# Two feed-forward blocks behind an attention: GpSimd kept to the attention, two-bank product tiles, one operation for both halves, and reordered products

## The chip, the cores and the metric

One core of one Trainium2 chip runs the kernel. The metric is the device time of one execution in microseconds. TensorE (PE, with its weight loads shown apart as PEld) multiplies, VectorE (DVE), ScalarE (ACT) and GpSimd (POOL) work element by element, and SyncE (SP) issues nearly all transfers.

## What is computed

```python
x = attention(q, k, v, w_phi)           # (2304, 512), feature-map attention
h = x @ w_in                            # w_in (512, 2048)
x = (relu(h) ** 2) @ w_out              # w_out (2048, 512)
gate = sigmoid(x @ w_gate)              # w_gate, w_val (512, 1536)
out = (gate * (x @ w_val)) @ w_out2     # w_out2 (1536, 512)
```

All inputs and outputs are fp32. The first block is called h below, the second gv.

## The kernel before

**Numbers in two parts.** Each fp32 operand of a matmul is split into a high part `hi` that TensorE takes and the rest `lo = a - hi`; three passes (hi·hi, hi·lo, lo·hi) make one product. ACT writes `hi` as a copy and another engine subtracts. For weights that is `wsplit` (L128): ACT at L131, the subtraction at L132 on POOL or DVE, as `on_pool` (L707) decides by the weight's name. For activations it is `split` (L85), with the subtraction on DVE at L90.

**Stages.** The 2304 tokens are three blocks of `TB` = 768 columns. The attention comes first. For token block 0, `h0_step` (L493) then multiplies directly with 16 pieces of `w_in`, and `o1_step` (L508) accumulates `g @ w_out` two steps behind it. For blocks 1 and 2 of the first feed-forward block, and for all three of the second, a `chain` of 2x2 block products with seven multiplications in place of eight makes `h`, or gate and value; 16 steps `o1` (first) or 12 steps `o2` (second) follow. One product is 12 matmuls of 384 columns; its two halves (m = 0, 1) have one PSUM bank each.

**A chain.** For each group q the seven products p1, p2, p6, p7, p5, p3, p4 (L600 to L626) go to three accumulators: X for p1, p6, p5, p3, Z for p2, Y for p7, p4. After p1, p6 and p5 `keep` (L569) has ACT copy both halves of X to scratch at L572, before the next product may add to X. After p2, p5 and p4 `joined` (L574) has DVE add Z or Y at L577; `squared` (L585) and `gated` (L595) make g of it. All this is done half by half.

**Around the products.** `xops` (L530) prepares the seven inputs of the next token block at one step of o1 or o2, its differences on POOL (L544). `g_split` (L632) splits a piece of g at the start of the step that uses it. While the h chains run, `weight` (L98) converts weights from their input format with four DVE operations (L105, L106, L107, L110) and one of ACT (L109), and `sums` (L152) adds and subtracts pieces of them on POOL (L156 to L159); the results go to DRAM and are fetched again.

**Order.** Each engine and each queue works strictly in its own order. The code's order is a proposal: a scheduler with a timeline of its own puts the instructions of each engine into a row when the kernel is built. `run_ahead(first[k], 11, 6)` (L712) fetches weights up to 11 products ahead and splits them up to 6 ahead.

**Buffers.** PSUM is one pool of eight single banks, `bank` (L56). `gx` has 16 tiles for g and its parts, `sc` 10 scratch tiles of one bank's size.

## Time and profile before

| | us |
|---|---|
| median of 3 runs | 1064.37 (1063.57 to 1067.43) |
| the profiled execution's own time | 1063.96 |
| its span, first to last instruction | 1062.1 |
| PE busy | 1006.6 |
| DVE busy | 805.9 |
| ACT busy | 590.3 |
| POOL busy | 496.3 |

The time outside the span is 1.86 us. A line such as L565 stands for all instructions of that line of the kernel. The idle time of an engine is counted before an instruction, with the instruction that ended the wait behind an arrow. An engine's busy time counts overlapping instructions once.

### The profile page before, as it was taken

What the parts mean: (1) busy time and instruction counts of PE and PEld (TensorE: products, weight loads), DVE (VectorE), ACT (ScalarE), POOL (GpSimd) and SP (SyncE); (2) the same over time, 40 slices, a digit from 0 to 9 for tenths busy, and PEclk for the clock granted to TensorE, in tenths of its full rate; (3) what the DMA queues carried; (4) which work ended last, traced back from release to release, by engine and by line L of the source; (5) the groups of instructions that cost most, each with busy time, mean ns of one, the idle gap of its engine ahead of it and who ended that gap; (6) DMA issues with size and microseconds to landing.
All of it is one profiled execution on the core that took longest, in us unless ns stands there. A gap on an engine that the chain in (4) does not pass through costs nothing.

```text
span 1062.1 us, 18013 instructions
## 1 busy us (share of the span) xinstructions
PE 1006.6 (95%) x6488; PEld 869.9 (82%) x6488; DVE 805.9 (76%) x1218; ACT 590.3 (56%) x1220; POOL 496.3 (47%) x486
## 2 busy tenths in 40 slices
PE   8999999899998997599997999999999999999997
PEld 6666666687876997488996889998899997899986
DVE  7899997599985999893899966999545687365650
ACT  7888878344434665343564436666345674365630
POOL 4555655534647657664558652129302265111430
PEclk9999999999999998799998999999999999999999
DMA  9445422058876565355572664772254432444401
GB/s 247 119 139 155 149 64 90 30 209 306 287 250 185 180 200 158 124 181 178 182 227 80 197 210 139 233 244 89 80 151 135 125 97 75 132 128 132 120 19 60
DMA packets 117849, 162.20 MB, mean 153 GB/s; under 512 B 12928, under 2 KB 75008, under 8 KB 117760
## 3 DMA queue, kind: packets, MB, share of 16 engines
q1 hardware_dynamic: 117120, 160.20, 48.4%
q8 instruction: 51, 0.84, 0.3%
q10 hardware_dynamic: 640, 0.85, 0.2%
q14 instruction: 38, 0.31, 0.1%
HBM read 127.99 MB, written 33.03 MB: 152 GB/s over the span
## 4 chain that ended last, share of the span: by engine, by line
PE 52%; DVE 8%; issue 1%; ACT 1%; DMA 0%; ACTq 0%; DVEq 0%
PE a L565 29%; PE a L660 12%; PE a L519 11%; DVE xs L90 3%; DVE glo L90 1%; DVE G L593 1%; DVE c L577 1%; DVE G L598 1%; DVE w L106 0%; DMA wf<-wd 0%; DVE w L105 0%; DVE hl L132 0%; DVE w L110 0%; ACT c L572 0%; DVE w L107 0%
## 5 line engine op out<-in xcount | busy, mean ns | idle before, releaser
L132 POOL TENSOR_TENSOR hl<-wf,hl 128x512 fp32r<-128x512 f32 x168 | 251.7, 1507 | 414.2 <-ACT hl L131 387.2
L565 PE MATMUL a<-xs,hl 128*128 128x384 f32 x2184 | 387.6, 340 | 9.1 <-DVE c L577 4.8
L565 PEld LDWEIGHTS a<-xs,hl 128*128 128x128 f32 x2184 | 383.2, 191 | 12.5 <-ACT c L572 6.0
L131 ACT ACTIVATE hl<-wf 128x512 fp32r<-128x512 f32 x282 | 172.2, 627 | 114.9 <-PE a L660 33.9
L519 PE MATMUL a<-ghi,hl 128*128 128x256 f32 (+1 forms) x768 | 194.6, 342 | 0.5 <-DVE ghi L89 0.5
L132 DVE TENSOR_TENSOR hl<-wf,hl 128x512 fp32r<-128x512 f32 x114 | 87.7, 777 | 95.7 <-ACT hl L131 95.5
L519 PE MATMUL a<-glo,hl 128*128 128x512 f32 (+1 forms) x384 | 131.6, 345 | 23.7 <-DVE glo L90 23.7
L519 PEld LDWEIGHTS a<-ghi,hl 128*128 128x128 f32 x768 | 135.8, 192 | 17.3 <-issue 0.9
L660 PE MATMUL a<-hl,ghi 128*128 128x512 f32 x432 | 132.4, 395 | 0.0
L577 DVE TENSOR_TENSOR c<-c,a 128x384 f32<-128x384 f32 x156 | 83.2, 549 | 37.4 <-ACT c L572 25.0
L109 ACT ACTIVATE st<-st 128x512 f32<-128x512 f32 x68 | 46.6, 686 | 106.7 <-DVE w L106 105.5
L572 ACT ACTIVATE c<-a 128x384 f32<-128x384 f32 x156 | 73.1, 487 | 55.1 <-PE a L565 54.7
L519 PEld LDWEIGHTS a<-glo,hl 128*128 128x128 f32 x384 | 74.0, 193 | 34.6 <-DVE glo L90 25.6
L660 PEld LDWEIGHTS a<-hl,ghi 128*128 128x128 f32 x432 | 81.1, 188 | 19.5
L311 POOL PARTITION_ALL_REDUCE m<-qe x64 | 82.0, 1351 | 29.0 <-ACT qe L309 29.0
L660 PE MATMUL a<-hl,glo 128*128 128x512 f32 x216 | 82.1, 396 | 1.5 <-DVE glo L90 1.5
L501 PE MATMUL a<-xs,hl 128*128 128x512 f32 (+1 forms) x384 | 72.9, 346 | 6.9 <-ACT c L504 6.2
L501 PEld LDWEIGHTS a<-xs,hl 128*128 128x128 f32 x384 | 60.5, 191 | 18.7 <-ACT c L504 8.5
L87 ACT ACTIVATE ghi<-G 128x768 fp32r<-128x768 f32 x48 | 40.2, 839 | 63.4 <-DVE glo L90 51.7
L90 DVE TENSOR_TENSOR glo<-G,ghi 128x768 fp32r<-128x768 f32 x48 | 57.8, 1206 | 16.3 <-ACT ghi L87 13.7
L106 DVE SCALAR_TENSOR_TENSOR w<-st,w 128x512 uint32<-128x512 uint32 x68 | 63.0, 927 | 0.8
L110 DVE SCALAR_TENSOR_TENSOR w<-st,w 128x512 f32<-128x512 f32 x68 | 57.1, 841 | 4.6 <-ACT st L109 2.1
(106 smaller groups left out, 1377.1 us busy)
## 6 DMA issues: line engine op xcount, KB each, us to landing
wf<-wd SPq DMA_DIRECT2D x84, 256.0 KB, 2.9
wf<-smd SPq DMA_DIRECT2D x72, 256.0 KB, 3.3
st<-in_moe_w_out_dram SPq DMA_DIRECT2D x28, 512.0 KB, 5.1
wf<-wid SPq DMA_DIRECT2D x56, 256.0 KB, 4.9
wf<-gvd SPq DMA_DIRECT2D x54, 256.0 KB, 3.2
st<-in_moe_w_in_dram SPq DMA_DIRECT2D x16, 512.0 KB, 5.5
wf<-ismd SPq DMA_DIRECT2D x32, 256.0 KB, 3.7
wd<-w SPq DMA_DIRECT2D x28, 256.0 KB, 2.6
```

The costliest lines, as they stand in the source:

```text
L90: last_g[0] = nc.vector.tensor_tensor(lo, src, f(hi), ALU.subtract)
L106: nc.vector.scalar_tensor_tensor(b, hi, 0xC0000000, b, ALU.bitwise_and, ALU.bitwise_or)
L110: nc.vector.scalar_tensor_tensor(a, h, TINY, a, ALU.is_ge, ALU.mult)
L131: nc.scalar.activation(d[:, 0], a, AF.Copy)
L132: eng.tensor_tensor(d[:, 1], a, f(d[:, 0]), ALU.subtract)
L311: nc.gpsimd.partition_all_reduce(m, a[:, 1, :], channels=P, reduce_op=bass_isa.ReduceOp.absmax)
L501: nc.tensor.matmul(pp, lhsT=w[:, x, j, :], rhs=xs[j][:, y, o:o + n], start=k == 0, stop=k == 3 * NJ - 1)
L519: nc.tensor.matmul(acc[j][i], lhsT=w[:, x, j, :], rhs=a[y][:, o:o + n], start=c == 0 and k == 0 and (i == 0 or j % 2 == 0), stop=c == C1 - ...
L565: nc.tensor.matmul(acc[k][m], lhsT=w[:, i, 2 * m + kt, :], rhs=v[:, j, kt, :], start=start and n == 0, stop=n == 5, skip_group_check=True)
L572: nc.scalar.activation(side[name][m], acc["X"][m], AF.Copy)
L577: last_g[0] = nc.vector.tensor_tensor(a[m], a[m], acc[k][m], ALU.add)
L660: nc.tensor.matmul(acc[u], lhsT=g[x][:, u * P:(u + 1) * P], rhs=w[:, y].rearrange("p j f -> p (j f)"), start=c == 0 and n == 0, stop=c == ...
```

## The change

- POOL no longer subtracts for `wsplit`, nor for `sums`, nor for the differences of a token block: DVE does all three. `on_pool` goes. POOL keeps its work in the attention.
- From the end of the attention PSUM is a pool `pd` of four tiles of two neighbouring banks, and both halves of a product lie in one of them. `keep`, the joins, the squares and the splits each become one operation over 2x384 columns. The accumulators are one per group q (`acc["X", q]`).
- In the first block the join and relu become one custom DVE operation, `TENSOR_ADD_SAT` (max(min(a + b, 3e38), 0)); ACT squares.
- In `h0_step` both halves have 384 columns (before 512 and 256); ACT writes the high part as a square, squares once more in fp32, and DVE subtracts once.
- p1 of the next group is written ahead of p3, and p2 of the next group behind p4.
- The inputs of the next token block are made one by one over seven steps (`xop`). `g_split` for step c + 2 stands behind step c, the first two some products ahead of the chain's end. `gx` shrinks from 16 to 4 tiles, `sc` is 7 tiles of two halves.
- Weights of the second block are converted at an even pace (`converts2`).

```diff
-    ps = ctx.enter_context(tc.tile_pool(name="ps", bufs=8, space=PSUM))
+    pctx = ctx.enter_context(ExitStack())
+    ps = pctx.enter_context(tc.tile_pool(name="ps", bufs=8, space=PSUM))
...
-        eng.tensor_tensor(d[:, 1], a, f(d[:, 0]), ALU.subtract)
+        nc.vector.tensor_tensor(d[:, 1], a, f(d[:, 0]), ALU.subtract)
...
-        eng = nc.gpsimd.tensor_tensor
+        eng = nc.vector.tensor_tensor
...
+    pctx.close()
+    pd = ctx.enter_context(tc.tile_pool(name="pd", bufs=4, space=PSUM, reuse_waits="tile"))
-    gx = ctx.enter_context(tc.tile_pool(name="gx", bufs=16, reuse_waits="tile"))
-    sc = ctx.enter_context(tc.tile_pool(name="sc", bufs=10, reuse_waits="tile"))
+    gx = ctx.enter_context(tc.tile_pool(name="gx", bufs=4, reuse_waits="tile"))
+    sc = ctx.enter_context(tc.tile_pool(name="sc", bufs=7, reuse_waits="tile"))
...
+        r, sq = scr(), scr()
+        nc.scalar.activation(r, pp[:, :, :NH], AF.Relu)
+        nc.scalar.activation(gs[c][0], flat(r), AF.Square)
+        nc.scalar.activation(sq, r, AF.Square)
+        last_g[0] = nc.vector.tensor_tensor(gs[c][1], flat(sq), f(gs[c][0]), ALU.subtract)
...
-                nc.gpsimd.tensor_tensor(d[kt], x[kt], y[kt], ALU.subtract)
+            nc.vector.tensor_tensor(d, x, y, ALU.subtract)
...
+            a = (xp if i < 4 else xb).tile([P, 2, 2, NH], F32R, tag=f"xo{i}", name="xs")
+            split(a[:, 0], a[:, 1], src, nc.scalar)
...
-        side[name] = [scr(NH) for m in range(2)]
-        for m in range(2):
-            nc.scalar.activation(side[name][m], acc["X"][m], AF.Copy)
+        side[name, q] = scr()
+        nc.scalar.activation(side[name, q], acc["X", q], AF.Copy)
...
+    def squared(q, e, j, k, name=None):
+        dst = g_pair(q, e)[:, :, j * NH:(j + 1) * NH]
+        if name is None:
+            r = scr()
+            nc.scalar.activation(r, acc[k, q], AF.Relu)
+        else:
+            r = side.pop((name, q))
+            last_g[0] = nc.vector._custom_dve(TENSOR_ADD_SAT, out=r, in0=r, in1=acc[k, q], s0=BIG, s1=0.0)
+        nc.scalar.activation(dst, r, AF.Square)
...
+            nc.vector.tensor_tensor(a, a, acc[k, q], ALU.add)
...
     def o1(t, c):
-        g_split(c)
         o1_step(t, c, take(("o1", t, c)))
+        g_ahead("h", c + 2)
...
+            order += [(p6, "s2", q), (p7, "s3", q), (p5, "s1", q)]
+            if q < n - 1:
+                order.append((p1, "a11", q + 1))
+            if q == n - 1:
+                order.append((p2, "a12", q))
+            order += [(p3, "s4", q), (p4, "a22", q)]
+            if q < n - 2:
+                order.append((p2, "a12", q + 1))
...
+    def g_ahead(kind, c):
+        if kind == "h" and c < C1:
+            q, r = divmod(c, 4)
+            g_split(c, q, *divmod(r, 2))
...
+        for i, (fn, k, q) in enumerate(order):
+            if i == len(order) - 7:
+                act(0.0, g_ahead, kind, 0)
+                act(0.0, g_ahead, kind, 1)
...
-            if c == C1 // 2:
-                act(0.0, xops, (t + 1) % nblk)
+            if 0 <= c - 3 < 7:
+                act(0.0, xop, (t + 1) % nblk, ORDER[c - 3])
...
-        upto = int(ngv * (at + 4) / (moe2 - 6)) if at < moe2 else ngv + int((at - moe2 + 4) / 3)
+        upto = int(NW2 * (at + 6) / (moe2 + 36))
```

Three places show how the rows of an engine move.

POOL, where the attention ends. Before, weight splits (`hl`, L132) and the sums of weights (`s`, L156 to L159) follow the attention's own `m` and `rc`:

```order
L311 ISA m<-qe 128x288 x4
L132 ISA
L132 TENSOR_TENSOR hl<-wf,hl 128x512 x3
L404 COPY rc<-rd 32x9 x8
L132 TENSOR_TENSOR hl<-wf,hl 128x512 x3
L404 COPY rc<-rd 32x9 x16
L132 TENSOR_TENSOR hl<-wf,hl 128x512 x4
L156 TENSOR_TENSOR s<-wf 128x256
```

After, these are POOL's last rows:

```order
L318 ISA m<-qe 128x288 x4
L411 COPY rc<-rd 32x9 x8
L318 ISA m<-qe 128x288 x4
L411 COPY rc<-rd 32x9 x24
L837 UNCONDITIONAL_BRANCH
L837 ISA
```

None of the splits and sums is left on POOL; they stand in DVE's row.

DVE in the first steps of o1 for token block 1. Before (`xs`: split of an input of the next block, `glo`: low part of g, `w`: conversion of a weight, `c`, `G`: joins and squares):

```order
L577 TENSOR_TENSOR c<-c,a 128x384
L90 TENSOR_TENSOR xs<-u,xs 128x384 x2
L593 SCALAR_TENSOR_TENSOR G<-c 128x384
L106 SCALAR_TENSOR_TENSOR w<-st,w 128x512
L90 TENSOR_TENSOR xs<-c,xs 128x384
L110 SCALAR_TENSOR_TENSOR w<-st,w 128x512
L593 SCALAR_TENSOR_TENSOR G<-c 128x384
L90 TENSOR_TENSOR xs<-c,xs 128x384 x3
L107 SCALAR_TENSOR_TENSOR w<-st,w 128x512
L90 TENSOR_TENSOR glo<-u,ghi 128x768
L90 TENSOR_TENSOR xs<-c,xs 128x384 x3
```

After, at the steps 4 to 6 of the same o1 (`c<-u`: difference of two pieces):

```order
L112 TENSOR_SCALAR w<-st 128x512
L97 TENSOR_TENSOR xs<-u,xs 128x768
L139 TENSOR_TENSOR hl<-wf,hl 128x512
L113 SCALAR_TENSOR_TENSOR w<-st,w 128x512
L114 SCALAR_TENSOR_TENSOR w<-st,w 128x512
L97 TENSOR_TENSOR glo<-G,ghi 128x768
L97 TENSOR_TENSOR xs<-u,xs 128x768
L112 TENSOR_SCALAR w<-st 128x512
L139 TENSOR_TENSOR hl<-wf,hl 128x512
L117 SCALAR_TENSOR_TENSOR w<-st,w 128x512
L113 SCALAR_TENSOR_TENSOR w<-st,w 128x512
L97 TENSOR_TENSOR glo<-G,ghi 128x768
```

A `glo` now stands behind every four to eight other operations, and the seven `xs` lie between them one at a time.

PE in the chain of token block 1, group 1. Before, from p5 to p4 (`a_5001` and `a_5002` are the halves of X, `a_5192` and `a_5193` Z of the next group's p2, `a_5070` and `a_5071` the halves of Y; `xs_4652`, `xs_4657` and `xs_4666` are the inputs of p5, p3 and p4):

```order
L565 MATMUL a_5001<-xs_4652,hl_4962 128x384 x6
L565 MATMUL a_5192<-xs_4625,hl_5067 128x384
L565 MATMUL a_5002<-xs_4652,hl_4962 128x384 x6
L565 MATMUL a_5192<-xs_4625,hl_5067 128x384 x3
L565 MATMUL a_5193<-xs_4625,hl_5067 128x384 x4
L565 MATMUL a_5001<-xs_4657,hl_4998 128x384 x6
L565 MATMUL a_5070<-xs_4666,hl_5021 128x384 x6
L565 MATMUL a_5002<-xs_4657,hl_4998 128x384 x6
```

After, the same group (`d_4832` is X, `d_5054` Z of the next group, `d_4980` X of the next group, `d_4940` Y; `xs_4556` is the input of p5, `xs_4606` of p3, `xs_4611` of p4):

```order
L590 MATMUL d_4832<-xs_4556,hl_4849 128x384 x12
L590 MATMUL d_5054<-xs_4331,hl_4937 128x384 x12
L590 MATMUL d_4832<-xs_4606,hl_4897 128x384 x12
L590 MATMUL d_4980<-xs_4415,hl_4955 128x384 x7
L590 MATMUL d_4940<-xs_4611,hl_4918 128x384 x12
```

Between p5 and p3 stood 7 matmuls of the next p2 after p5's last one; now all 12 of it stand there, and p5 is one row of 12.

## Rows read from the trace of the kernel before

**Rows 1.** The page: the span, and busy time by engine.

```profile
span 1062.1 us, 18013 instructions
PE 1006.6 (95%) x6488; PEld 869.9 (82%) x6488; DVE 805.9 (76%) x1218; ACT 590.3 (56%) x1220; POOL 496.3 (47%) x486
```

**Rows 2.** Busy time in seven stages: PE, PEld, DVE, ACT, POOL, granted clock, DMA.

```profile
0.00:196.98 196.98, 188.61 (x2121) 124.80 (x2121) 164.65 (x363) 156.18 (x385) 111.79 (x188) 1.00 0.46 134
196.98:350.45 153.47, 141.34 (x770) 120.58 (x769) 128.44 (x180) 63.91 (x126) 82.52 (x82) 0.97 0.65 216
350.45:500.39 149.94, 132.56 (x723) 121.48 (x723) 126.05 (x145) 74.05 (x142) 89.83 (x69) 0.93 0.56 177
500.39:639.83 139.44, 129.51 (x722) 119.75 (x721) 119.55 (x140) 71.81 (x135) 84.38 (x62) 0.98 0.55 174
639.83:780.04 140.21, 138.79 (x721) 127.81 (x721) 110.72 (x165) 82.14 (x160) 49.28 (x32) 1.00 0.48 153
780.04:918.88 138.84, 138.05 (x722) 127.86 (x721) 85.73 (x123) 75.22 (x146) 45.95 (x32) 1.00 0.38 114
918.88:1062.10 143.22, 137.77 (x720) 127.59 (x719) 70.76 (x106) 66.96 (x128) 32.53 (x23) 0.99 0.34 101
```

**Rows 3.** The chain that ended last, pieces without a wait: start, us, work.

```profile
586.23 53.60 PE a L519 x306
918.88 87.37 PE a L565 x504
1006.25 50.42 PE a L660 x216
```

**Rows 4.** Timeline of PE: start, us, work, idle before and its releaser.

```profile
260.37 2.23 PE L501 MATMUL a<-xs,hl 128*128 128x512 f32 x6 [2.52 <-ACT c L504]
...
344.58 0.58 PE L519 MATMUL a<-glo,hl 128*128 128x256 f32 x1 [4.82 <-DVE glo L90]
...
440.19 0.79 PE L519 MATMUL a<-glo,hl 128*128 128x512 f32 x1 [11.31 <-DVE glo L90]
...
573.48 0.50 PE L519 MATMUL a<-glo,hl 128*128 128x512 f32 x1 [3.05 <-DVE glo L90]
```

**Rows 5.** Timelines of DVE ahead of 440.19 and of ACT ahead of 260.37.

```profile
434.00 3.60 DVE L90 TENSOR_TENSOR xs<-c,xs 128x384 fp32r<-128x384 f32 x3
437.54 1.21 DVE L107 SCALAR_TENSOR_TENSOR w<-st,w 128x512 uint32<-128x512 uint32 x1
438.67 1.47 DVE L90 TENSOR_TENSOR glo<-u,ghi 128x768 fp32r<-128x768 f32 x1
...
259.15 0.68 ACT L109 ACTIVATE st<-st 128x512 f32<-128x512 f32 x1 [3.89 <-DVE w L106]
```

**Rows 6.** Instructions of single lines: duration in ns least/median/most, start of first and last.

```profile
L132 POOL TENSOR_TENSOR hl<-wf,hl x168: 1259/1476/2295, 188.3 to 1032.2; 128x512 fp32r<-128x512 f32 x168
L132 DVE TENSOR_TENSOR hl<-wf,hl x114: 675/687/1781, 333.5 to 992.8; 128x512 fp32r<-128x512 f32 x114
L577 DVE TENSOR_TENSOR c<-c,a x156: 533/548/556, 356.6 to 1008.6; 128x384 f32<-128x384 f32 x156
L593 DVE SCALAR_TENSOR_TENSOR G<-c x36: 545/1075/1651, 371.9 to 569.2; 128x384 f32<-128x384 f32 x36
L90 DVE TENSOR_TENSOR glo<-G,ghi x48: 944/959/2046, 446.7 to 1027.1; 128x768 fp32r<-128x768 f32 x48
L90 DVE TENSOR_TENSOR xs<-c,xs x40: 544/1073/1651, 342.6 to 887.8; 128x384 fp32r<-128x384 f32 x40
L105 DVE TENSOR_SCALAR w<-st x68: 411/454/1523, 38.2 to 714.6; 128x512 uint32<-128x512 uint32 x68
L106 DVE SCALAR_TENSOR_TENSOR w<-st,w x68: 670/692/1782, 39.9 to 716.0; 128x512 uint32<-128x512 uint32 x68
L87 ACT ACTIVATE ghi<-G x48: 826/845/852, 445.8 to 1026.0; 128x768 fp32r<-128x768 f32 x48
```

**Rows 7.** Waits: engine and line, waited for, us in total, times, longest.

```profile
ACT c L572 <- PE a L565: 54.7, 81, 2.2
```

More of the change, by code (lines that the diff above doesn't have):

```diff
@@ L8 @@
 from concourse._compat import with_exitstack
+from concourse.dve_ops import TENSOR_ADD_SAT
 F32 = mybir.dt.float32
@@ L93, in xsplit @@
         a = xp.tile([P, 2, TB], F32R, tag=f"xo{j}", name="xs")
-        for o, n in SUBS:
-            split(a[:, 0, o:o + n], a[:, 1, o:o + n], xy[0, j][:, o:o + n])
+        for o, n in HALVES:
+            split(a[:, 0, o:o + n], a[:, 1, o:o + n], xy_tile(0, j)[:, o:o + n])
         xs[j] = a
@@ L200, in split_in @@
         if s < C1 and ("in", s) not in ws:
[L201 removed]
+            wsplit(("in", s), fetched.pop(("in", s)))
     def split_out(s):
[L204 removed]
+        wsplit(("out", s), fetched.pop(("out", s)))
     with ExitStack() as actx:
@@ L495, in h0_step @@
         gs[c] = pair()
-        for o, n in SUBS:
-            pp = bank(n)
+        pp = dbl()
+        for i, (o, n) in enumerate(HALVES):
             k = 0
@@ L500, in h0_step @@
                 for x, y in passes:
[L501 removed]
+                    nc.tensor.matmul(pp[:, i, :n], lhsT=w[:, x, j, :], rhs=xs[j][:, y, o:o + n], start=k == 0, stop=k == 3 * NJ - 1)
                     k += 1
[L503 to L506 removed]
+        r, sq = scr(), scr()
[3 more added lines that the diff above has]
+        last_g[0] = nc.vector.tensor_tensor(gs[c][1], flat(sq), f(gs[c][0]), ALU.subtract)
     def o1_step(t, c, w):
         if c == 0:
[L510 to L511 removed]
+            wide = [dbl() for d in range(2)]
+            thin = dbl()
             for j in range(NJ):
[L513 to L514 removed]
+                acc[j] = wide[j // 2][:, j % 2], thin[:, j // 2, j % 2 * 256:j % 2 * 256 + 256]
+            acc["o"] = wide, thin
+            for d in range(NJ // 2):
+                xy.pop((t, d))
         a = gs.pop(c)
@@ L522, in o1_step @@
         if c == C1 - 1:
-            for j in range(NJ):
-                for i, (o, n) in enumerate(SUBS):
-                    nc.scalar.activation(xy_tile(t, j)[:, o:o + n], acc[j][i], AF.Copy)
+            wide, thin = acc["o"]
+            for d in range(NJ // 2):
+                u = xy_pair(t, d)
+                nc.scalar.activation(u[:, :, :512], wide[d], AF.Copy)
+                nc.vector.tensor_copy(u[:, :, 512:], thin[:, d].rearrange("p (k n) -> p k n", k=2))
     side = {}
     G = {}
-    def xops(t):
+    ORDER = ("B11", "B21", "T2", "T1", "T4", "T3", "B22")
@@ L531, in h, with xop @@
+    HOME = ("T3", "T1", "B22", "T4", "B11", "B21", "T2")
+    diff = {}
+    def xop(t, k):
         def h(d, j):
-            return [xy[t, 2 * d + kt][:, j * NH:(j + 1) * NH] for kt in range(2)]
-        def put(k, src):
-            i = ("T3", "T1", "B22", "T4", "B11", "B21", "T2").index(k)
-            a = (xp if i < 4 else xb).tile([P, 2, 2, NH], F32R, tag=f"xo{i}", name="xs")
-            for kt in range(2):
-                split(a[:, 0, kt], a[:, 1, kt], src[kt], nc.scalar)
-            xs[k] = a
@@ L557, in product @@
+        xs[k] = a
     def product(k, key, x, start):
+        q = key[2]
         w, v = take(key), xs[x]
         if start:
-            acc[k] = [bank(NH) for m in range(2)]
+            acc[k, q] = dbl()[:, :, :NH]
         for m in range(2):
@@ L686, in chain @@
     def chain(kind, n, dat, sm, end, t):
+        order = [(p1, "a11", 0), (p2, "a12", 0)]
         for q in range(n):
-            for fn, k in ((p1, "a11"), (p2, "a12"), (p6, "s2"), (p7, "s3"), (p5, "s1"), (p3, "s4"), (p4, "a22")):
-                act(1.0, fn, (kind, t), q, end, need=[(((kind, t), k, q), lambda k=k, q=q: sources(dat, sm, q)[k])])
+            order += [(p6, "s2", q), (p7, "s3", q), (p5, "s1", q)]
[10 more added lines that the diff above has]
+                act(0.0, g_ahead, kind, 1)
+            act(1.0, fn, (kind, t), q, end, need=[(((kind, t), k, q), lambda k=k, q=q: sources(dat, sm, q)[k])])
     for t in range(1, nblk):
```

151 lines of the change are left out of this document (73 added, 78 removed).

## The prediction

> **What bounds the kernel now.** I read the page first: PE is busy for 1006.6 of 1062.1 us [rows 1], so it is the bound, and only time that PE loses can be won. Where it loses time the table of stages tells, against what each stage needs when nothing disturbs it. Three pieces of the chain of waits give PE's undisturbed pace [rows 3]: 504 matmuls of a product in 87.37 us, 173.4 ns each; 306 of o1 in 53.60 us, 175.2 ns each; 216 of o2 in 50.42 us. The direct product of block 0 has o1's mean width, so it gets o1's pace. This makes a floor:
>
> - attention up to the first matmul of h0: 196.98 us, as it is [rows 2];
> - block 0 of h, 384 + 384 matmuls: 768 x 0.1752 = 134.5;
> - blocks 1 and 2 of h, 28 products of 12 and 384 of o1 each: 336 x 0.1734 + 384 x 0.1752 = 125.5, twice 251.0;
> - three blocks of gv: 87.37 + 50.42 = 137.8, three times 413.4;
> - after PE's last matmul, at 1006.25 + 50.42 = 1056.67 us: 5.4.
>
> Together 1001.3 us. The span is 60.8 us over it, and the stages say where [rows 2]: block 0 of h takes 153.47 (19.0 over), block 1 149.94 (24.4 over), block 2 139.44 (13.9 over), the three gv blocks 2.4, 1.0 and 0.0 over. So 57.3 us lie in the h blocks. [...]
>
> What PE waits for: four of its longest waits are 11.31, 4.82 and 3.05 us for `glo` of DVE (L90) and 2.52 us for an evacuation by ACT [rows 4]. Behind each stands a slow DVE. Ahead of the wait of 11.31 us DVE takes 3.60 us for three operations on 128x384, 1.20 each, and 1.21 and 1.47 for the next two [rows 5]. Ahead of the 2.52 us, ACT is idle for 3.89 us at L109 for a weight conversion of DVE (L106), and the evacuation at L504 is behind that in ACT's row [rows 5]. The same operations have a least time of half and less: 544 ns against a median of 1073 for 128x384, 944 against 2046 at most for 128x768, 670 against 1782 [rows 6]. Only the join at L577, which takes one operand from PSUM, is always the same, 533 to 556 [rows 6]. In the h stages POOL is busy for 82 to 90 us, each of its weight splits 1476 ns at the median [rows 2, 6]. I read that as DVE operations on two SBUF operands stretched while POOL works: the waits are POOL's, though POOL is on no chain.
>
> **POOL's work goes to DVE.** 168 weight splits at 687 ns (DVE's median for the same) add 115 us, 80 operations of the sums on 128x256 at no more than 128x384's 544 ns add 44, 20 differences on 128x768 at 944 add 19 [rows 6]: 178 us more for DVE. Against it the stretch goes, and fusion takes off instructions. Whether DVE then holds PE up is asked stage by stage, with least or median times and every instruction that the built order has in the stage.
>
> Block 1 or 2 of h: 14.5 weights converted at 0.411 + 3 x 0.692 = 2.49 (36.1 us); 24 operations of sums at 0.544 (13.1); 44 weight splits at 0.687 (30.2); 12 fused joins at 0.944 (11.3), 16 splits of g (15.1), 11 operations for the next inputs (10.4); two evacuations of some 0.69 (1.4). Sum 117.6 of 125.5 us. Successive DVE operations overlap: one starts at 438.67 while the one before ends at 437.54 + 1.21 = 438.75 [rows 5]. 0.08 for each of some 167 operations takes off 13: 104 us, 83%. Block 0 by the same account: 22 conversions (54.7), 32 sums (17.4), 36 weight splits (24.7), 16 of h0 (15.1), 11 for the inputs (10.4), 1.4: 123.7, less 0.08 x 185, is 109 of 134.5 us, 81%. The first gv block of before ran with DVE busy for 110.72 of 140.21 us, 79%, and lost 2.4 us [rows 2]. So DVE stays below PE, near a load that is known to cost little.
>
> **Wide operations.** ACT's copy of 128x768 takes 845 ns [rows 6]; I take it for every wide evacuation and square. ACT gets 24 squares (20 us) and 16 squares in block 0 more, but has only some 64 to 74 us of work in the h stages [rows 2], so they stay hidden in about 85 of 125.5 us. The fused custom operation is not in the trace. Its nearest row is the DVE operation with two inputs on 128x768, 944 ns least; its upper bound are the four instructions that it replaces, 2 x 548 + 2 x 545 = 2.2 us [rows 6]; less than 0.944 would need fewer passes over the same data, and no row has that. I take 0.944, by shape. The upper end adds 12 x 1.25 = 15 us of DVE per block, which would make 119 of 125.5: then I count some 8 us lost per block, 16 in all, for the range.
>
> **Reordering and PSUM.** The order shows the next p2 between p5 and p3 before, too, only by halves: PE's matmuls change little, and products cost it nothing extra. The evacuation of X can now start only when both halves are done; 12 matmuls, 2.08 us, cover its 0.845. Spread inputs and splits of g two steps ahead cost no operation and take the burst of `xs` off DVE ahead of a `glo`. Nothing for either beyond what the waits give.
>
> **SP and transfers.** The fetches keep their number; they wait for a weight buffer to come free, now by DVE's 687 ns and not POOL's 1476. Nothing.
>
> [...] The second gv block has PE with weight loads for 127.86 of 138.84 us, 92%, and loses 1.0 us [rows 2]; the floor above stands on that pace. [...]
>
> **The sum.** Forecast: the three h blocks lose 2.4 us each, as the first gv block does, and the first two gv blocks 1.0 each: 9.2. Span 1001.3 + 9.2 = 1010.5; with the 1.86 us outside the span 1012.4 against the profiled 1063.96. The median is 0.41 above that execution, so the prediction is 1012.8. No wait left at all would give 1003.6.
>
> **Rivals.**
>
> 1. *Thin buffers bring waits back.* `gx` falls to two pairs: the split for step c + 2 can start only when step c has ended, and its 0.845 on ACT and 0.944 on DVE [rows 6] must fit into step c + 1, 24 x 0.1752 = 4.2 us. 2.4 us are spare. The order puts up to eight other DVE operations, some 4 us, between two splits. For: DVE at 83% has no reserve in that step. Against: 2.4 us are three operations. If DVE is one operation, 0.69, late at each of the 32 steps of o1, 22 us come back: 1035.
> 2. *Slower: evacuation on PE's path.* 78 copies of X (3 of each of 26 groups) now wait for the whole product. Should ACT stand in front of each with other work, as weight splits, so that it comes 1 us after its cover, PE waits 78 us: 1013 + 78 = 1091. It decides from a lateness of (1064 - 1013) / 78 = 0.65 us. For: ACT has one row, and more latency in each operation. Against: today ACT waits for PE at 81 of the 156 copies, 54.7 us in all [rows 7], so it is early at half of them, and the cover leaves 1.2 us. [...]
> 3. *It isn't POOL.* If the stretch of DVE has another source that stays (the transfers, say), DVE would need half as much again and be over PE's time in the h blocks: 104 x 1.5 = 156 per block is what block 1 takes today. The time would be about 1064. Against: the join at L577 never stretches in the same stages [rows 6], and gv, with POOL at a third, hardly loses.
> 4. *The change does less than it says.* The built order has POOL without a split, 78 wide copies and 24 fused joins; this is out.
>
> **Chances.** Forecast 0.75, rival 1 0.14, rival 2 0.06, rival 3 0.04, others 0.01. Differences within 0.5% are about what a measurement of this kernel can't tell from no change. Faster by more than that: forecast and rival 1, 0.89; the same 0.04; slower 0.07. The range goes from no wait left, 1003.6, to just over rival 1, 1036, which holds the dear end of the fused join, 1013 + 16 = 1029, too.
>
> **What would show it.** Right: POOL idle after 197 us; DVE's subtraction at a median of 687 with a most under 750; the three h blocks at 136 to 139 and 127 to 130 us with a granted clock of 0.99 and more; no wait of PE for `glo` over 2 us. Rival 1: waits of PE for `glo` (L97) at many steps of o1. Rival 2: PE waiting for ACT at the wide copy. Wrong on the fused join: over 1.2 us each. Rival 3: DVE's medians still at 1.0 us and more for 128x384's work.

## The result, and the profile after

The changed kernel takes 1027.19 us (median of 4 executions, 1025.64 to 1027.74), against 1063.97 us for the kernel before in the same session: a ratio of 0.9645, 95% interval 0.9622 to 0.9668. The forecast was 1012.8 us in a range from 1003.6 to 1036. The sign and the range hold; the gain is 37 us where 51 were forecast. The profiled execution took 1027.08 us, its span 1025.3.

The page of the changed kernel, span and busy time by engine; its counterpart is [rows 1]:

```profile
span 1025.3 us, 17544 instructions
PE 992.4 (97%) x6488; PEld 870.3 (85%) x6488; DVE 746.6 (73%) x1283; ACT 601.0 (59%) x1081; POOL 109.4 (11%) x198
```

PE is the bound still, and lost 14 us of busy time. POOL has nothing to do behind the attention. DVE took over POOL's splits, sums and differences and is busy for 59 us *less* than before.

Its stages, each cut at the first matmul behind the mixed steps at a stage's end (span, then busy time of PE, PEld, DVE, ACT, POOL, granted clock, DMA share, GB/s), the counterpart of [rows 2]:

```profile
204.26:349.13 144.87, 139.44 (x781) 129.71 (x782) 106.36 (x183) 73.53 (x109) 0.00 (x0) 0.98 0.72 240
349.13:475.50 126.37, 126.37 (x725) 117.70 (x725) 108.40 (x176) 79.57 (x118) 0.00 (x0) 1.00 0.63 204
475.50:602.80 127.30, 126.40 (x724) 117.44 (x723) 101.26 (x162) 77.21 (x116) 0.00 (x0) 1.00 0.62 202
602.80:741.50 138.70, 137.80 (x720) 127.64 (x719) 99.63 (x152) 77.30 (x129) 0.00 (x0) 1.00 0.45 140
741.50:880.50 139.00, 138.10 (x721) 127.94 (x719) 86.24 (x126) 72.64 (x122) 0.00 (x0) 1.00 0.38 114
880.50:1025.30 144.80, 135.86 (x706) 125.34 (x705) 74.62 (x112) 64.94 (x111) 0.00 (x0) 0.98 0.33 99
```

In block 1 of h PE is busy without a gap, 126.37 of 126.37 us, in block 2 for 126.40 of 127.30, both at a granted clock of 1.00; DVE stands at 86% and 80% beside it. In the changed kernel the first products of a chain are mixed with the last steps before it, so these cuts shift some 3 us between neighbours. For a comparison the stages are cut below by PE's count of matmuls (at numbers 2120, 2888, 3608 and 4328), which is the same work in every kernel:

| us | before | floor | forecast | after | after, over the floor |
|---|---|---|---|---|---|
| attention | 197.0 | 197.0 | 197.0 | 204.3 | 7.3 |
| h, block 0 | 153.5 | 134.5 | 136.9 | 142.0 | 7.5 |
| h, block 1 | 149.7 | 125.5 | 127.9 | 126.5 | 1.0 |
| h, block 2 | 139.4 | 125.5 | 127.9 | 127.0 | 1.5 |
| gv, with the tail | 422.5 | 418.8 | 420.8 | 425.6 | 6.8 |
| span | 1062.1 | 1001.3 | 1010.5 | 1025.3 | 24.0 |

Over the floor lie 24.0 us where 9.2 were forecast. Against the forecast the attention lost 7.3 us more, block 0 of h 5.1 and gv 4.8; blocks 1 and 2 of h took 2.3 less. The waits of PE name the largest part of the first two (engine and line, what was waited for, us in total, times, longest):

```profile
PE a L245 <- POOL ident masks.py:199: 9.8, 1, 9.8
PE d L538 <- DVE glo L523: 5.1, 1, 5.1
PE d L590 <- ACT c L596: 3.6, 4, 0.9
PE d L517 <- DVE u L417: 1.7, 1, 1.7
```

**The start.** Before, the same first wait was 1.6 us. POOL's timeline at the start of the changed kernel:

```profile
0.72 0.20 POOL masks.py:197 MEMSET ident<- 128x128 f32 x1 [0.29 <-POOLq L826]
9.43 0.28 POOL masks.py:199 TENSOR_SCALAR_AFFINE_SELECT ident<-ident 128x128 f32<-128x128 f32 x1 [8.51 <-issue]
```

POOL stands for 8.51 us and waits for nothing that the profile shows; the memset just ahead of it is not late. In the kernel before, the same instruction starts at 1.22 us.

**The end of block 0.** DVE's timeline ahead of PE's wait of 5.07 us:

```profile
333.83 0.43 DVE L163 TENSOR_TENSOR s<-wf 128x256 f32<-128x256 f32 x1 [4.00 <-DMA wf<-wid]
...
339.54 0.42 DVE L163 TENSOR_TENSOR s<-wf 128x256 f32<-128x256 f32 x1 [4.16 <-DMA ismd<-s]
...
342.10 0.95 DVE L523 TENSOR_TENSOR glo<-c,ghi 128x768 fp32r<-128x768 f32 x1
```

DVE is not slow here. It stands twice in front of a sum of `w_in`, first for the fetch of its input (`wf<-wid`), then for the store of the sums before (`ismd<-s`, since `sp` has one tile). The split of g that PE needs is behind both in DVE's row. Of the 7.5 us that block 0 takes over its floor, this wait is 5.1. Behind it the granted clock is 0.50 from 343 to 347 us and 0.79 to 349, then 1.00 (in the kernel before, behind the wait of 11.31 us, 0.50 from 440.2 to 444.2). Before, POOL did these sums and did the waiting.

**The tail.** From PE's last matmul to the end it takes 8.0 us, before 5.4. ACT's timeline there (its queue's transfers are ACTq):

```profile
1015.43 0.39 ACT L705 ACTIVATE c<-d 128x256 f32<-128x256 f32 x1 [5.92 <-PE d L694]
1016.31 0.38 ACTq L707 DMA_DIRECT2D out_dram<-c  x1
1016.74 0.66 ACT L705 ACTIVATE c<-d 128x256 f32<-128x256 f32 x2 [0.92 <-DVE c L703]
1017.61 1.42 ACTq L707 DMA_DIRECT2D out_dram<-c  x2
1019.08 0.66 ACT L705 ACTIVATE c<-d 128x256 f32<-128x256 f32 x2 [1.69 <-issue]
1019.95 0.96 ACTq L707 DMA_DIRECT2D out_dram<-c  x2
1020.96 0.38 ACT L705 ACTIVATE c<-d 128x256 f32<-128x256 f32 x1 [1.22 <-DVE c L703]
```

PE ends at 1017.26. The last copies come in pairs now, two pieces to a two-bank tile, the first 1.8 us ahead of PE's end where it was 3.5 before, and transfers issued by ACT stand between them. No experiment takes this one apart. The runs narrow it down: the tail is 5.7 us in *dve_alone* (below), which keeps the single banks, and 8.0 to 8.2 in *lib_back* and *pool_back*, which have the rest of the change.

The durations that the forecast took are met (ns, least/median/most): DVE's weight split, 687 as in [rows 6] with a most of 699 in place of 1781, the 128x768 split, and the fused join:

```profile
L139 DVE TENSOR_TENSOR hl<-wf,hl x282: 647/687/699, 188.1 to 993.6; 128x512 fp32r<-128x512 f32 x141
L97 DVE TENSOR_TENSOR glo<-G,ghi x48: 950/959/960, 418.8 to 1009.5; 128x768 fp32r<-128x768 f32 x48
L610 DVE CUSTOM_DVE_ANT_1 c<-c,d x24: 948/954/956, 353.6 to 536.6; 128x768 f32<-128x768 f32 x24
```

### The profile page after: what moved, and what is told of

The parts are those of the page before. It is cut to its first block, busy times and chain, and to the rows that moved or that the text cites. A ratio compares the mean times of both kernels' runs of the same rounds, so it can differ in the third digit from the quotient of the medians.

```text
span 1025.3 us, 17544 instructions
## 1 busy us (share of the span) xinstructions
PE 992.4 (97%) x6488; PEld 870.3 (85%) x6488; DVE 746.6 (73%) x1283; ACT 601.0 (59%) x1081; POOL 109.4 (11%) x198
## 4 chain that ended last, share of the span: by engine, by line
PE 85%; DVE 6%; DMA 4%; ACT 2%; issue 2%; POOL 0%; ACTq 0%; SPq 0%; POOLq 0%; DVEq 0%
PE d L590 37%; PE d L538 17%; PE d L694 15%; PE d L517 4%; PE a L360 3%; DMA wf<-wid 2%; PE a L397 2%; PE a L334 2%; PE a L367 1%; PE a L390 1%; PE a L313 1%; DMA st<-in_moe_w_in_dram 1%; PE a L292 1%; DVE km L339 1%; PE a L377 1%
## 5 line engine op out<-in xcount | busy, mean ns | idle before, releaser
L590 PE MATMUL d<-xs,hl 128*128 128x384 f32 x2184 | 385.5, 337 | 3.6 <-ACT c L596 3.6
L590 PEld LDWEIGHTS d<-xs,hl 128*128 128x128 f32 x2184 | 379.5, 188 | 6.7 <-ACT c L596 4.9
L139 DVE TENSOR_TENSOR hl<-wf,hl 128x512 fp32r<-128x512 f32 x282 | 192.5, 688 | 76.4 <-ACT hl L138 75.3
L538 PE MATMUL d<-ghi,hl 128*128 128x256 f32 (+1 forms) x768 | 191.9, 340 | 0.0
L538 PEld LDWEIGHTS d<-ghi,hl 128*128 128x128 f32 x768 | 133.0, 190 | 16.4
L538 PE MATMUL d<-glo,hl 128*128 128x512 f32 (+1 forms) x384 | 130.0, 342 | 5.1 <-DVE glo L523 5.1
L694 PE MATMUL d<-hl,ghi 128*128 128x512 f32 x432 | 126.7, 395 | 0.0
L694 PEld LDWEIGHTS d<-hl,ghi 128*128 128x128 f32 x432 | 80.9, 188 | 18.2
L97 DVE TENSOR_TENSOR glo<-G,ghi 128x768 fp32r<-128x768 f32 x48 | 46.0, 958 | 57.3 <-ACT ghi L94 56.9
L538 PEld LDWEIGHTS d<-glo,hl 128*128 128x128 f32 x384 | 73.1, 190 | 14.1 <-DVE glo L523 5.4
L694 PE MATMUL d<-hl,glo 128*128 128x512 f32 x216 | 76.3, 395 | 0.0
L517 PE MATMUL d<-xs,hl 128*128 128x384 f32 x384 | 69.2, 337 | 2.1 <-DVE u L417 1.7
L517 PEld LDWEIGHTS d<-xs,hl 128*128 128x128 f32 x384 | 66.6, 188 | 3.8 <-DVE u L417 2.2
```

The source lines that it names most:

```text
L97: last_g[0] = nc.vector.tensor_tensor(lo, src, f(hi), ALU.subtract)
L139: nc.vector.tensor_tensor(d[:, 1], a, f(d[:, 0]), ALU.subtract)
L517: nc.tensor.matmul(pp[:, i, :n], lhsT=w[:, x, j, :], rhs=xs[j][:, y, o:o + n], start=k == 0, stop=k == 3 * NJ - 1)
L538: nc.tensor.matmul(acc[j][i], lhsT=w[:, x, j, :], rhs=a[y][:, o:o + n], start=c == 0 and k == 0 and (i == 0 or j % 2 == 0), stop=c == C1 - ...
L590: nc.tensor.matmul(acc[k, q][:, m], lhsT=w[:, i, 2 * m + kt, :], rhs=v[:, j, kt, :], start=start and n == 0, stop=n == 5, skip_group_check ...
L694: nc.tensor.matmul(acc[u], lhsT=g[x][:, u * P:(u + 1) * P], rhs=w[:, y].rearrange("p j f -> p (j f)"), start=c == 0 and n == 0, stop=c == ...
```

## The experiments

Theory A is on the start: what one execution ran last on POOL decides how long POOL stands at the start of the next, 8.51 us in the changed kernel and 0.29 in the kernel before. The expectations speak of code, or a library, that stays loaded; that is the author's reading, and the runs show the waits alone. Theory B is on block 0: DVE's row stands behind transfers. The contention theory is the prediction's own: POOL stretches DVE's operations. Stages are by matmul counts, as in the table.

### The start: one POOL instruction more at the end

In the changed kernel POOL's row ends with an all-reduce and 24 copies (`rc`) behind it. *lib_back* is that kernel with an addition behind the copies:

```diff
+            if n == B * NJ - 1:
+                z = xy_tile(nblk - 1, NJ - 1)[:, TB - 32:]
+                nc.gpsimd.tensor_tensor(dum, z, z, ALU.add)
```

> The changed kernel with one more GpSimd operation, an addition on 128x32 whose result nobody uses, behind the last operation of the attention. In the changed kernel GpSimd stands still from 0.97 to 9.43 us, and the attention behind it. Theory A: the addition and the reduction of the attention need different code on GpSimd, what was loaded last stays for the next execution, and the changed kernel now ends with the reduction's; the addition at the end puts the first code back, so the selection starts near 1.2 us and the time falls by 8 us, from 1027.2 to 1019. Rival B: the custom VectorE operation, or something else at the start of the changed kernel, holds GpSimd: the gap stays, 1027.

Measured: 1019.6 us (1019.44 to 1020.55), ratio 0.9565 (0.9543 to 0.9587). An added instruction made the kernel 7.6 us faster. *lib_away* is the kernel before, with the opposite done to it in its last stage:

```diff
+        if t == nblk - 1 and c == C2 - 5:
+            nc.gpsimd.partition_all_reduce(scr(32), f(ws[("o2", t, C2 - 1)][:, 1, 0])[:, :32], channels=P, reduce_op=bass_isa.ReduceOp.absmax)
```

> The kernel before with one more reduction on GpSimd over 128x32, of which nobody uses the result, behind its last weight split. Theory A: GpSimd now ends with the reduction's code, so the next execution starts with a gap of some 8 us like that of the changed kernel: 1064 + 8 = 1072. Rival B: no gap, 1064, since nothing of the custom operation is in it.

Measured: 1071.98 us (1070.94 to 1073.96), ratio 1.0053 (1.0036 to 1.0071), 5.6 us over the 1066.42 of the kernel before in the same session, where 8 were expected; in the profiled execution the attention takes 206.9 us in place of 197.0. POOL's first selection in *lib_back*, then in *lib_away*:

```profile
1.21 0.36 POOL masks.py:199 TENSOR_SCALAR_AFFINE_SELECT ident<-ident 128x128 f32<-128x128 f32 x1 [0.29 <-POOL ident masks.py:197]
```

```profile
10.14 0.28 POOL masks.py:199 TENSOR_SCALAR_AFFINE_SELECT ident<-ident 128x128 f32<-128x128 f32 x1 [9.22 <-issue]
```

The added addition of *lib_back* pays the price itself, where nothing waits for it:

```profile
203.19 0.23 POOL L482 TENSOR_TENSOR dum<-u 128x32 f32<-128x32 f32 x1 [6.98 <-issue]
```

Theory A holds from both sides, with one limit that the rows show. Additions, subtractions and the selection are one kind, the all-reduce is the other, and copies and memsets belong to neither: the 24 copies between the last all-reduce and this addition did not spare it the 6.98 us, in the attention copies and all-reduces alternate without such a pause (in the kernel before, of the 13 all-reduces behind a copy the quickest starts after 0.35 us, each released by ACT), and at the start of the changed kernel the memset comes after 0.29 us, the selection behind it after 8.51. What the next execution pays at its start is set by which of the two kinds came last on POOL, and not by the last instruction of its row: 8.51 and 9.22 us where it was the all-reduce (the changed kernel, *lib_away*), 0.29 where it was an addition or a subtraction (*lib_back*, the kernel before). The experiment *noise*, below, shows the same price inside one execution.

### Is it POOL's contention, or its lateness?

*pool_back* undoes the move alone: weight splits, sums and differences are on POOL again, all else is as in the changed kernel.

```diff
-        nc.vector.tensor_tensor(d[:, 1], a, f(d[:, 0]), ALU.subtract)
+        (nc.gpsimd if on_pool(key) else nc.vector).tensor_tensor(d[:, 1], a, f(d[:, 0]), ALU.subtract)
...
-        eng = nc.vector.tensor_tensor
+        eng = nc.gpsimd.tensor_tensor
...
-            nc.vector.tensor_tensor(d, x, y, ALU.subtract)
+            nc.gpsimd.tensor_tensor(d, x, y, ALU.subtract)
```

> The changed kernel with the weight splits that GpSimd had, the sums of weights and the differences of a token block put back on GpSimd; tiles, fusion and order stay as changed, and the gap at the start goes since GpSimd ends with a subtraction. Theory (GpSimd's work stretches VectorE's): VectorE's operations on two SBUF operands have medians of 1.0 us and more again, TensorE waits for the low parts of g, and the time is at least 17 us above the same kernel without that (1019 by theory A): 1036 to 1050. Rival (fusion and wider operations brought the gain): within 3 us of 1019.

Measured: 1046.84 us (1042.09 to 1047.48), ratio 0.9809 (0.9778 to 0.984), 27 over *lib_back*, which has the same start. Blocks 1 and 2 of h take 141.0 and 133.3 us (*lib_back* 126.4 and 127.0). The expected medians of 1.0 us and more came only in part: the weight splits that DVE keeps have a median of 685 ns, with a most of 1820, the splits `xs<-c` of 128x768 one of 1845. PE's waits:

```profile
PE d L595 <- ACT c L601: 8.1, 5, 4.5
PE d L543 <- DVE glo L97: 6.7, 5, 1.9
PE d L595 <- POOL hl L144: 2.4, 3, 1.6
```

The last of them is POOL's own lateness and makes 2.4 us. *dve_alone* does the move alone, in the kernel before (with the addition of *lib_back*):

```diff
-        eng.tensor_tensor(d[:, 1], a, f(d[:, 0]), ALU.subtract)
+        nc.vector.tensor_tensor(d[:, 1], a, f(d[:, 0]), ALU.subtract)
...
-        eng = nc.gpsimd.tensor_tensor
+        eng = nc.vector.tensor_tensor
...
-                nc.gpsimd.tensor_tensor(d[kt], x[kt], y[kt], ALU.subtract)
+                nc.vector.tensor_tensor(d[kt], x[kt], y[kt], ALU.subtract)
```

> The kernel before with all of GpSimd's work behind the attention put on VectorE, and nothing else of the change; one unused addition on GpSimd at the end of the attention, so that no gap at the start comes in. Theory: this is most of the gain, VectorE's medians fall to their least, the time is 1020 to 1035; what is above 1019 is the price of the narrow operations (24 joins and 24 squares of 128x384 in a block of h in place of 12 fused ones, 15 us of VectorE). Rival: VectorE becomes the bound without the fusion, and the time stays at 1050 or more.

Measured: 1024.27 us (1022.43 to 1025.15), ratio 0.9605 (0.9581 to 0.9629). So the move without wide operations, fusion or reordering makes most of the gain, and all of the rest only 4.7 us more (to 1019.6); against the changed kernel with its late start (1027.19) it is not slower. The shares depend on the order in which they are counted: with POOL's work kept, the rest alone gains 19.6 us (*pool_back*, from 1066.42 in that session). But both runs leave a rival: POOL's splits are slow, and others wait for them. *noise* has POOL work that nobody waits for and that reads nothing of the kernel, in *lib_back*:

```diff
+    idle = dm.tile([P, 192], F32, name="idle")
+    nc.gpsimd.memset(idle, 0.0)
+    for _ in range(340):
+        nc.gpsimd.tensor_tensor(idle, idle, idle, ALU.subtract)
```

> lib_back with 340 subtractions on 128x192 added on POOL behind the attention, on a tile of zeros of their own: they read nothing of the kernel, and nothing waits for them. Contention theory (it is the stretch of DVE's operations, and not POOL's lateness, that costs): POOL works without a break from some 200 us for 200 to 270 us, that is through blocks 0 and 1 of h; in that time DVE's subtraction L139, 0.687 us in lib_back, takes 0.9 to 1.3, and the two blocks get 10 to 25 us longer each (lib_back 141.6 and 126.4 by PE's matmul counts), while block 2 of h, where POOL is idle again, stays at 127; 1035 to 1065 us. Rival (what was dear in the kernel before were POOL's own slow splits, which others waited for): DVE's times and all stages stay as in lib_back, 1018 to 1021 us.

Measured: 1383.73 us (1379.27 to 1385.96), far over both expectations, for a reason that belongs to theory A. The scheduler put 63 of the subtractions into the attention, between the all-reduces. POOL's timeline there:

```profile
42.10 0.50 POOL L501 TENSOR_TENSOR idle<-idle 128x192 f32<-128x192 f32 x1 [6.97 <-issue]
48.61 3.72 POOL L319 PARTITION_ALL_REDUCE m<-qe  x3 [6.00 <-issue]
59.45 0.50 POOL L501 TENSOR_TENSOR idle<-idle 128x192 f32<-128x192 f32 x1 [7.12 <-issue]
65.91 3.72 POOL L319 PARTITION_ALL_REDUCE m<-qe  x3 [5.97 <-issue]
```

Each change from one kind to the other costs 6 to 7 us in which POOL stands with nothing to wait for: 28 changes to the subtraction at a median of 7.13 us, 28 back at 5.96. The attention takes 516.7 us in place of 197.1. The way to the subtraction is a good 1 us longer than the way back. In the kernel before a pair of `MODIFY_POOL_CONFIG` stands in POOL's queue at the first selection (1.1 us), at the first all-reduce (1.5) and at the first weight split (180.7), and at the copies of L404 none. That the price reaches from one execution into the next is what *lib_back* (0.29 us) and *lib_away* (9.22) add.

Behind the attention the run answers the question it was made for. Its three h blocks (columns as above):

```profile
516.70:691.40 174.70, 146.29 (x768) 134.05 (x769) 150.84 (x179) 73.36 (x110) 158.08 (x215) 0.92 0.62 197
691.40:828.50 137.10, 130.42 (x723) 119.48 (x722) 123.19 (x176) 78.39 (x117) 48.76 (x65) 0.97 0.59 185
828.50:955.50 127.00, 126.10 (x722) 117.22 (x721) 102.28 (x164) 77.15 (x115) 0.00 (x0) 1.00 0.64 203
```

With 158 us of POOL work block 0 takes 174.7 us (*lib_back* 141.6), with 49 us block 1 takes 137.1 (126.4), with none block 2 takes the same 127.0. DVE's groups in *noise* from 520 to 740 us (busy, mean ns):

```profile
L139 DVE TENSOR_TENSOR hl<-wf,hl 128x512 fp32r<-128x512 f32 x48 | 46.4, 984 | 14.3 <-ACT hl L138 14.3
L112 DVE TENSOR_SCALAR w<-st 128x512 uint32<-128x512 uint32 x27 | 17.7, 663 | 1.1 <-DMA st<-in_moe_w_in_dram 0.9 <-DMA st<-in_moe_w_out_dram 0.2
L532 DVE TENSOR_TENSOR glo<-c,ghi 128x768 fp32r<-128x768 f32 x16 | 19.5, 1218 | 0.8 <-ACT c L531 0.4 <-ACT ghi L530 0.3
L619 DVE CUSTOM_DVE_ANT_1 c<-c,d 128x768 f32<-128x768 f32 x7 | 6.6, 941 | 0.0
```

The subtraction goes from 687 to 984 ns, the join that reads PSUM stays at its 0.94 to 0.95 us. The contention theory holds: POOL's activity alone, on no chain, costs PE tens of us, 33 in block 0 (expected were 10 to 25) and 11 in block 1.

The rows say more on the kind of the price. In *noise* a DVE operation gets 0.24 to 0.30 us longer at the mean whether it takes 0.42 us alone (663 less 422), 0.69 (984 less 687) or 0.95 (1218 less 955), beside POOL operations that take 0.50 us in the attention and 0.75 here. In the kernel before, beside POOL splits of 1.26 us and more, the longest of each kind but the join lies 1.10 to 1.11 us over its least, from 411 to 1523 ns and from 944 to 2046 alike [rows 6]. I read that as one wait for each operation, set by the length of POOL's operation, and not as a slower pace. By this, fewer and wider DVE operations pay less beside POOL, which would fit the 19.6 us above. Both are estimates from these rows; no run tests them.

### The end of block 0

*sums_gp* gives the results of these sums six tiles of a free pool, in *lib_back*, so that none waits for the store before:

```diff
-        sums(*ab, wsm[q][:, :, m])
+        t = gp.tile([P, 2, TB], F32, tag="g", name="G").rearrange("p a b -> p (a b)")[:, :4 * HF]
+        sums(*ab, wsm[q][:, :, m], t.rearrange("p (s f) -> p s f", s=4))
```

> The changed kernel with the small GpSimd addition behind the attention (as in lib_back) and one more edit: the results of the sums of w_in (L163 to L166, called for the inputs of the first block's chain) go to the free tiles of the pool gp, six of them, where they had one tile that is shared by all. In lib_back PE waits 5.0 us for glo at the end of block 0 of h, and DVE's row ahead of it stands 4.1 us for the store of the previous sums (ismd<-s). Theory B (DVE's row waits for that one tile): the wait for the store goes, PE's wait falls to under 1.5 us, and the slow clock behind it goes; block 0 of h gets 5 to 9 us shorter, 1011 to 1015 us. Rival (the fetch of w_in, wf<-wid, holds the row back, and the store only lies beside it): DVE then waits for the fetch in the same place, PE's wait stays at 3 to 5 us, 1017 to 1020.

Measured: 1017.75 us (1016.74 to 1018.08), ratio 0.956 (0.9539 to 0.958). DVE's timeline:

```profile
325.83 0.43 DVE L164 TENSOR_TENSOR G<-wf 128x256 f32<-128x256 f32 x1 [3.77 <-DMA wf<-wid]
...
329.44 0.42 DVE L164 TENSOR_TENSOR G<-wf 128x256 f32<-128x256 f32 x1 [2.06 <-DMA wf<-wid]
```

The wait for the store is gone, and a shorter one for the fetch came out from behind it; PE's wait falls from 5.0 to 2.6 us and block 0 from 141.6 to 138.3. Both theories have half. *in_pool* puts these 32 operations on POOL again, in the changed kernel:

```diff
-        sums(*ab, wsm[q][:, :, m])
+        sums(*ab, wsm[q][:, :, m], nc.gpsimd.tensor_tensor)
```

> The changed kernel with one part undone: the 32 operations of the sums of w_in (L163 to L166, called for the first block's chain) are on POOL again, all the other work stays on DVE; POOL's last instruction is then a subtraction, not the all-reduce. Theory B (in block 0 DVE's row stands behind transfers, for the fetch and for the store of these sums): PE's wait for glo at the end of block 0 falls from 5.0 us to under 1, block 0 of h takes 136 to 138.5 us by matmul counts (lib_back 141.6), POOL does the waiting; theory A gives 197 us for the attention; together 1013 to 1016.5 us. Rival (32 operations of POOL stretch DVE enough to take it back): block 0 stays at 140 to 143, 1018 to 1022 us.

Measured: 1020.95 us (1018.84 to 1022.55), ratio 0.9582 (0.9559 to 0.9605). Block 0 falls to 134.3 us, its floor, and block 1 takes 132.9 in place of 126.4. ACT's timeline at the border:

```profile
337.29 0.63 ACT L138 ACTIVATE hl<-wf 128x512 fp32r<-128x512 f32 x1 [8.49 <-DMA wf<-wid]
337.82 0.79 ACT L595 ACTIVATE c<-d 128x768 f32<-128x768 f32 x1
```

PE's timeline behind it:

```profile
338.67 52.06 PE L589 MATMUL d<-xs,hl 128*128 128x384 f32 x288 [5.03 <-ACT c L595]
```

POOL takes 0.7 to 1.5 us for an operation of the sums where DVE takes 0.42. In SP's queue the next fetch of a weight (`wf<-wid`, L196) stands behind the store of the sums (L166), which goes out only when POOL has done them, at 332.49:

```profile
332.52 0.57 SPq L166 DMA_DIRECT2D ismd<-s  x1
333.18 0.59 SPq L196 DMA_DIRECT2D wf<-wid  x1
```

So the weight comes late, ACT waits for it, and the evacuation that PE needs is next in ACT's row. Nearly all of the 7 us only moved over the border, and the time misses the 1013 to 1016.5 of theory B. *early* leaves the sums on DVE and calls each two steps earlier (in *burst*, below):

```diff
-        if s >= 3 and s % 2 and s <= C1 + 1:
-            for i in range(C1 // 2):
-                if i == (s - 3) // 2:
-                    in_sums(i)
+        if s % 2 and s < C1:
+            in_sums((s - 1) // 2)
```

> burst with one more edit: each of the eight sums of w_in for the first block's chain is called one odd step (two steps of block 0) earlier, on DVE as in burst, so that the last one is no longer ahead of the last splits of g in block 0. Theory B (the row of DVE stands behind transfers at the end of block 0, and nothing else is late there): PE's wait for glo, 3.8 us in burst, falls to under 1, block 0 of h falls from 139.4 to 135 to 137 us by matmul counts, block 1 stays at 126.4; 1011 to 1013.5 us against 1015.9. Rival (the end of block 0 is short of fetch buffers and of SP's row, so that the wait only moves, as it did in in_pool): block 0 gets shorter and block 1 longer, or block 0 stays; 1015 to 1019 us.

Measured: 1012.1 us (1011.07 to 1013.86), ratio 0.9513 (0.9489 to 0.9537), against 1015.87 for *burst*. PE's waits in *early* have none for `glo` any more:

```profile
PE d L521 <- DVE u L418: 2.5, 1, 2.5
PE d L594 <- ACT c L600: 1.8, 2, 0.9
PE a L246 <- POOL ident masks.py:199: 1.6, 1, 1.6
```

Block 0 falls from 139.4 to 136.7 us, block 1 stays (126.4, then 125.8). Theory B holds in this: the place of these sums in DVE's row was the fault, and called earlier they hold nothing up. The intervals of *early* and *burst* still touch; the stages show the difference where the edit is. This kernel beats both the kernel before and the changed one.

### The other parts of the change

*no_custom* splits the fused operation into DVE's addition and ACT's relu:

```diff
-            last_g[0] = nc.vector._custom_dve(TENSOR_ADD_SAT, out=r, in0=r, in1=acc[k, q], s0=BIG, s1=0.0)
+            last_g[0] = nc.vector.tensor_tensor(r, r, acc[k, q], ALU.add)
+            nc.scalar.activation(r, r, AF.Relu)
```

> The changed kernel with its fused custom operation (L610) put back into two instructions: DVE adds, ACT takes relu; nothing else, so the addition of lib_back is not in it. Theory A (POOL's first instruction of another library comes late because the all-reduce of the attention is the last that the execution before left loaded): the idle 8.5 us at POOL's start stay, and the time is 1025 to 1031. Rival (the custom DVE operation in the program makes the start late): POOL's start is as before, 1.2 us, and the time falls to 1018 to 1022. On the fusion itself: 24 more operations of ACT, 0.8 each, hidden behind PE, so at most 3 us more than the changed kernel; a loss of over 5 us would show that the fusion carries part of the gain.

Measured: 1028.34 us (1027.45 to 1029.73), ratio 0.9662 (0.964 to 0.9684); the changed kernel has 0.9645 (0.9622 to 0.9668). The fusion is worth 1 to 2 us, no more than the intervals leave open; by stages block 2 of h takes 2.9 us more without it and block 0, where the edit has nothing, 3.0 less, so the stages leave room for some 3 us. The late start has nothing to do with it: PE's first wait is still 9.6 us. *old_order* writes the products in the order of before, in *lib_back*:

```diff
-        order = [(p1, "a11", 0), (p2, "a12", 0)]
...
+        order = [(fn, k, q) for q in range(n) for fn, k in ((p1, "a11"), (p2, "a12"), (p6, "s2"), (p7, "s3"), (p5, "s1"), (p3, "s4"), (p4, "a22"))]
```

> lib_back with the products of each chain written in the order of the kernel before (p1, p2, p6, p7, p5, p3, p4 for every group). If the scheduler already puts the next group's p2 where the new text has it: 1018 to 1022 us, against 1019.6 for lib_back. If the written order carries part of the gain, because the next product then waits for an accumulator or a join: PE waits at p2 or p1 for ACT or DVE, some 0.5 to 1 us at each of 22 changes of group, 1030 to 1040.

Measured: 1032.84 us (1030.55 to 1034.31), ratio 0.9701 (0.9675 to 0.9727), 13 over *lib_back*. The main wait of PE in *lib_back*'s order, then in this one:

```profile
PE d L594 <- ACT c L600: 3.6, 4, 0.9
```

```profile
PE d L594 <- ACT c L600: 12.4, 15, 0.9
```

PE waits for the wide copy at eleven more places, 8.8 of the 11.1 us by which the two profiled executions differ; fourteen of the 15 stand 84 matmuls or a multiple of that behind a chain's start, where a group of seven products ends. Everything else of the change in the old order is dearer than none of it (*dve_alone*, 1024.27). So the reordering is what the wide copies need; a run with the new order and narrow copies, which would separate the two, is missing. *burst* makes the seven inputs of the next token block at one step, as before, in *lib_back*:

```diff
-            if 0 <= c - 3 < 7:
-                act(0.0, xop, (t + 1) % nblk, ORDER[c - 3])
+            if c == C1 // 2:
+                for o in ORDER:
+                    act(0.0, xop, (t + 1) % nblk, o)
```

> lib_back with all seven inputs of the next token block made at one step of o1 or o2, where the kernel before has them, in place of one each at seven steps. The burst is eleven DVE operations of 0.95 us, some 10 us, against 4.2 us for a step of o1. If DVE's work ahead of a split of g holds PE up: one PE wait for glo (L97) of 2 to 6 us in each of five token blocks, 10 to 25 us more with the clock, 1030 to 1045. If the scheduler puts the split ahead of the burst in DVE's row: 1018 to 1023.

Measured: 1015.87 us (1013.27 to 1017.0), ratio 0.9541 (0.9512 to 0.9571), below both expectations. Spreading the inputs gains nothing; its interval still overlaps that of *lib_back* (0.9543 to 0.9587). Two of the four waits of 0.90 us are gone in it. *best* joins *burst* and *in_pool*.

> in_pool and burst together: the sums of w_in on POOL, the seven inputs of the next token block made at one step, and the small POOL addition of lib_back. If the two gains are separate (burst 1015.9 against lib_back's 1019.6, in_pool some 4 us): 1008 to 1013 us, faster than both kernels. If burst's difference was the chip's scatter: as in_pool, 1013 to 1017 us.

Measured: 1018.84 us (1018.49 to 1020.1), ratio 0.9565 (0.9547 to 0.9584), over both expectations. Block 0 took 135.8 us and block 1 135.6: the wait moved as in *in_pool*, and the two gains are not separate.

## Why the prediction was right, and where it was not

**Right: POOL's work goes to DVE.** POOL's activity was the cause of DVE's stretch (*noise*), its removal most of the gain (*dve_alone*), and DVE at 80 to 86% (83% were forecast) leaves PE with hardly a gap: blocks 1 and 2 lose 1.0 and 1.5 us where 2.4 were forecast. One detail was too narrow. I tied the stretch to two operands in SBUF; the conversion with a single one (`TENSOR_SCALAR`) goes from 422 to 663 ns as well, and [rows 6] had it already, with 411 to 1523 at L105. In the same stretch of *noise* the fused join, with an operand in PSUM, stays: 941 ns at the mean, 952 in *lib_back*.

**Right: wide operations.** ACT's wide copy has a median of 0.812 us (taken: 0.845), the fused join 0.954 (0.944). The dear end of 2.2 was far off.

**Wrong: "attention up to the first matmul of h0: 196.98 us, as it is".** It took 7.3 us more. The step costed what the change does inside an execution; it left out that with POOL's splits gone the all-reduce is the last of the two kinds on POOL, the copies behind it changing nothing, and that the next execution's selection then starts after 8.51 us of idle POOL in place of 0.29. The kernel before had the price in it, too: POOL's first split behind the attention comes at 188.3 us [rows 6], 7.5 us after its pair of `MODIFY_POOL_CONFIG`, and other work covered it. (The page names a copy of ACT as what ended that wait; in *pool_back* the same place has 6.86 us with nothing named.)

**Wrong: "SP and transfers … Nothing."** The fetches do keep their number. But this step looked at buffers, and not at who stands behind a wait. The sums were counted as 0.544 us of DVE each (they take 0.42); that with them DVE's row inherits POOL's waits for fetch and store, with the split of g behind them, was in no term. So block 0 lost 7.5 us, 2.4 forecast.

**Wrong: gv, "1.0 each" and 5.4 of tail.** It lost 4.8 us more than forecast. Of its 6.8 over the floor 2.6 are in the tail, where two-bank tiles pair the last copies (read from the rows, not tested), 2.7 in three waits of 0.90 us, the rest in smaller ones. I had costed wide operations in the chains only.

**The reordering: "products cost it nothing extra".** True of the order as it stands, but the term was not a nothing: with wide copies, 13 us are lost without it (*old_order*).

**Rivals.** 1, thin buffers, did not come: no wait of PE for `glo` (L97) is among its waits. 2, evacuation on PE's path, is at work in small: four waits of 0.90 us, and 15 without the reordering. 3, it isn't POOL, is refuted by *noise*. What made the time longer than forecast was in none of them. So the range held by luck: its upper part was there for rival 1 (1035) and for a dear fused join (1029), neither of which came, and 1027 lies in it for other reasons. Of the signs named for being right three failed, all in block 0: 142.0 us where 136 to 139 were named, a granted clock of 0.98 where 0.99 was, and a wait for `glo` of 5.1 us where none over 2 was to be.

Two readings in the prediction were off without bearing on the forecast. 156 us is not what block 1 took, that was 149.94 [rows 2]. And the four waits of PE that it lists are not the four longest: one for DVE's join had 4.0 us, one for ACT's copy at L572 2.8.

*early*, which is the changed kernel without the late start and the wait in block 0, takes 1012.1 us, next to the 1012.8 forecast, but that does not make the forecast better: 5 us of gv over its floor are still in it, and h's blocks 1 and 2 are better than forecast.

## What to carry over

When work moves from one engine to another, its waits move with it: list what each moved instruction waits for, and what stands behind it in its new row, before adding up durations. Price a slow neighbour by what it does to others, for which a run with work that nobody needs is a clean test. And look at what an engine ran last in an execution: here POOL's wait at the start of the next one hung on it, 8.51 us or 0.29.
